# Half of the first matrix product by seven quarter products that share two PSUM banks, and exponentials laid out by key blocks

## The chip, the cores and the metric

The kernel runs on one core of a Trainium2 chip. The metric is the device time of one execution in microseconds (us). Single instructions are given in us or ns. The engines are PE (TensorE; PEld is its weight loads), DVE (VectorE), ACT (ScalarE), POOL (GpSimd) and SP (SyncE, which here only issues DMAs).

## What is computed

All data are float32. `q`, `k`, `v` are 8 batches x 8 heads x 576 rows x 64; the model width is 512, the hidden width 2048.

```python
scores = scale * q @ k.T
thresh = max(scores, -1) - tau
attn = softmax(where(scores >= thresh, scores, -1e9)) @ v
x = attn.transpose(0, 2, 1, 3).reshape(B, S, H * D)     # 8 x 576 x 512
xn = (x - mean(x)) / sqrt(var(x) + 1e-6) * g_ln
out = x + maximum(xn @ w_ch1, 0) @ w_ch2
```

## The kernel before

**Attention** runs in 72 slots (9 to a batch). A slot computes 4 blocks of 128 query rows x 576 keys. PE makes the scores in PSUM (L405). DVE takes the row maxima (L419), ACT makes four exponentials (L432) into a room in SBUF, DVE masks and sums them (L439), and POOL divides (L455). From slot 6 on (`by_blocks`) the weights are turned without PE: two DVE transposes of 32x32 blocks copy the room `e` into a second tile `et` (L529), SP writes `et` to DRAM (L540, four pieces at L536 in the first batch), and reads it back in a new layout as `em` and `er` (L554, L559). The product with the values (L598, L608) is issued in the slot after. From slot 7 on all slots use the same room, `e_room[0]`. A room is free for the next slot's exponentials when it has been copied to `et`.

**The feed-forward part** runs in 16 groups of 288 tokens. The first part (`first_part`) makes 16 feature tiles of 128 x 288: each is 4 products over the model width, one PSUM bank, and one ReLU on ACT (L796) into `hidden`. `product` (L101) issues every product as two of 64 columns; each shows as two PE records, so that a tile has 16 records of 288 columns. Of the rows' scale `rb`, the squares (L802), their sum on POOL (L804) and a `var` product lie among the tiles. In groups 1 to 15 the second part (`second_quarters`) already forms its 2x2 block product by seven quarter products with sums of blocks (the Winograd form of Strassen's method). Each of the seven is a segment of 64 records of 144 columns into one bank, then one ACT copy (L887); sums of blocks are made on DVE and POOL (L872, L912). Group 0's second part is plain. All products of both parts, and `mean` and `var`, take turns in two PSUM banks (tag `ff`).

**The order** is written by hand. A slot is cut in four quarters; `second_part(n, i)` issues as many feed-forward steps as a budget (`ROOM`, `STEPS`) gives to the quarter. PE, ACT, DVE and POOL execute in the order of issue. Quarter 0 follows the scores: maxima, exponentials 0 and 1, the quarter's products, exponentials 2 and 3. The masks and the divisions are issued after quarter 1, the transposes and the DMA after quarter 2, the values' product before quarter 3.

**The start.** The weights arrive as chunks of 512 columns that ACT, DVE and POOL convert (L278 to L313) in the first eleven slots, in spare pieces of SBUF (`Weights`). POOL ends each chunk (L308).

## Time and profile before

| what | value |
|---|---|
| median of 3 runs | 1347.15 us (1347.1 to 1347.81) |
| the profiled execution, first to last instruction | 1345.5 us |
| DVE, ACT, POOL busy, share of the span | 65%, 34%, 46% |
| one maximum, exponential, mask, division | 1351, 754, 810, 792 ns |
| one ReLU of a tile, one copy of a segment | 416, 403 ns |
| one transpose of half a room | 1373 ns |
| DMA of a room to DRAM (L540), issue to landing | 4.8 us (4.1 to 6.5) |

The span is the time from the first to the last instruction of one profiled execution; it lies 1.65 us under the median of the runs. The profile was taken on another execution than the timed ones. Means are over all instructions of a group. PE records overlap, so PE's rate is read from runs of records in the chain of waits and not from the length of one record.

### The profile page before, as it was taken

The numbers are of one execution on the slowest core, as the hardware profiler recorded it, in microseconds if no ns is written. First come the engines' busy times: TensorE is split into PE (matmuls) and PEld (weight loads), VectorE is DVE, ScalarE is ACT, GpSimd is POOL, SyncE is SP. The second block draws the span as 40 slices with busy tenths as digits, with TensorE's granted clock in tenths as the row PEclk, the third lists the DMA queues.
The fourth block names the chain that finished last, engine by engine and source line by source line (L and its number), as shares of the span: only waits on it lengthen the run. The fifth ranks groups of instructions, "written<-read, shape, count | busy, mean of one in ns | idle before, by whom it ended". The sixth has DMA issues, their size and how long they took to land.

```text
span 1345.5 us, 40255 instructions
## 1 busy us (share of the span) xinstructions
PE 1313.5 (98%) x17304; PEld 989.7 (74%) x17304; DVE 870.6 (65%) x1544; ACT 458.7 (34%) x995; POOL 621.9 (46%) x836
## 2 busy tenths in 40 slices
PE   8898899999999999999999999999999999999997
PEld 7665567769686776868778696877869677786957
DVE  7879886667666675666756677656756667666112
ACT  5866333232323233232233324233232323333120
POOL 3475556534444444445535454443444445335312
PEclk9999999999999999999999999999999999999999
DMA  8937874557643775447734576447754476443211
GB/s 173 297 95 176 209 191 151 178 163 190 176 146 132 182 200 158 151 156 200 191 127 150 167 183 191 139 137 196 198 167 152 126 196 179 136 157 124 81 19 20
DMA packets 335298, 213.92 MB, mean 159 GB/s; under 512 B 247376, under 2 KB 292688, under 8 KB 327056
## 3 DMA queue, kind: packets, MB, share of 16 engines
q1 hardware_dynamic: 329008, 210.46, 54.6%
q8 instruction: 136, 2.23, 0.7%
q10 hardware_dynamic: 5952, 0.74, 0.4%
q0 software_dynamic: 160, 0.15, 0.1%
q14 instruction: 42, 0.34, 0.1%
HBM read 124.00 MB, written 87.29 MB: 157 GB/s over the span
## 4 chain that ended last, share of the span: by engine, by line
PE 91%; ACT 3%; DVE 2%; DMA 1%; POOL 1%; issue 1%; SPq 1%; POOLq 0%; ACTq 0%; DVEq 0%
PE p L101 38%; PE seg L101 31%; PE sc L405 10%; PE sc L598 9%; PE sc L608 2%; ACT e L432 1%; PE tp L101 1%; DVE e L439 1%; POOL w L308 1%; PE var L101 1%; PE mean L101 1%; SPq L118 0%; DMA scr<-et 0%; ACT em L489 0%; DMA k_in<-in_k_dram 0%
## 5 line engine op out<-in xcount | busy, mean ns | idle before, releaser
L101 PE MATMUL p<-xc,w 128*64 128x288 f32 x4096 | 517.1, 408 | 6.5 <-ACT part L887 4.6
L101 PEld LDWEIGHTS p<-xc,w 128*64 128x64 f32 x4096 | 287.7, 137 | 213.8 <-issue 13.5
L419 DVE TENSOR_REDUCE neg<-sc 128x2 f32<-128x1152 f32 x144 | 188.7, 1351 | 282.2 <-PE sc L405 281.6
L455 POOL TENSOR_SCALAR e<-e,den 128x576 f32<-128x576 f32 x264 | 205.9, 792 | 131.3 <-DVE den L444 131.3
L101 PE MATMUL seg<-hidden,w 128*64 128x144 f32 x3840 | 247.9, 287 | 0.0
L101 PEld LDWEIGHTS seg<-hidden,w 128*64 128x64 f32 x3840 | 234.9, 137 | 11.5 <-issue 8.5
L439 DVE SCALAR_TENSOR_TENSOR e<-sc,thr,e 128x576 f32<-128x576 f32 x288 | 222.4, 810 | 19.3 <-POOL thr L423 11.6
L423 POOL TENSOR_SCALAR thr<-neg,low_sb 128x2 f32<-128x2 f32 x144 | 39.4, 274 | 384.1 <-DVE neg L419 382.4
L796 ACT ACTIVATE hidden<-p 128x288 f32<-128x288 f32 x256 | 106.5, 416 | 305.3 <-PE p L101 303.7
L432 ACT ACTIVATE e<-sc,neg 128x576 f32<-128x576 f32 x288 | 197.6, 754 | 2.4 <-DVE neg L419 2.4
L529 DVE STREAM_TRANSPOSE et<-e 128x1152 f32<-128x1152 f32 x118 | 161.1, 1373 | 14.2 <-POOL e L455 13.7
L405 PE MATMUL sc<-kT,qT 64*64 64x384 f32 (+3 forms) x2048 | 140.3, 403 | 3.1 <-DVE e L439 3.1
L598 PE MATMUL sc<-em,v_in 128*64 128x128 f32 (+1 forms) x2368 | 130.9, 264 | 2.4 <-DVE w L293 2.4
L598 PEld LDWEIGHTS sc<-em,v_in 128*64 128x64 f32 x2368 | 124.0, 138 | 10.9 <-DVE w L293 2.6
L101 PE MATMUL seg<-hidden,stage 128*64 128x144 f32 x1920 | 123.3, 286 | 0.0
L101 PEld LDWEIGHTS seg<-hidden,stage 128*64 128x64 f32 x1920 | 117.6, 137 | 2.9 <-issue 2.9
L621 ACT COPY x<-sc 128x128 f32<-128x128 f32 x120 | 31.6, 265 | 245.2 <-PE sc L405 176.3
L405 PEld LDWEIGHTS sc<-kT,qT 64*64 64x64 f32 x2048 | 76.3, 133 | 44.6 <-issue 21.3
L872 POOL TENSOR_TENSOR hidden<-hidden 128x576 f32<-128x576 f32 x60 | 84.8, 1427 | 52.0 <-ACT hidden L796 42.4
L887 ACT COPY part<-seg 128x288 f32<-128x288 f32 x74 | 29.8, 403 | 190.6 <-PE seg L101 190.1
L872 DVE TENSOR_TENSOR hidden<-hidden 128x576 f32<-128x576 f32 x60 | 51.2, 887 | 51.5 <-PE seg L101 48.5
L101 PE MATMUL seg<-hidden,e 128*64 128x144 f32 x896 | 61.2, 286 | 0.0
(130 smaller groups left out, 1041.2 us busy)
## 6 DMA issues: line engine op xcount, KB each, us to landing
scr<-et SPq DMA_DIRECT2D x63, 1152.0 KB, 4.8
em<-scr SPq DMA_DIRECT2D x63, 1024.0 KB, 5.7
out_dram<-ot SPq DMA_DIRECT2D x248, 36.0 KB, 3.8
q_in<-in_q_dram SPq DMA_DIRECT2D x120, 72.0 KB, 2.7
er<-scr SPq DMA_DIRECT2D x132, 64.0 KB, 5.2
k_in<-in_k_dram SPq DMA_DIRECT2D x116, 72.0 KB, 3.0
v_in<-in_v_dram SPq DMA_DIRECT2D x28, 256.0 KB, 5.4
w<-in_moe_w_ch_dram SPq DMA_DIRECT2D x10, 512.0 KB, 7.0
```

The costliest lines, as they stand in the source:

```text
L101: nc.tensor.matmul(out[r], lhsT=lhsT[:, r], rhs=rhs, **flags)
L405: nc.tensor.matmul(sc[h][64 * i : 64 * i + 64, at : at + n], lhsT=ql[r] if s == HP else qT[r, half, j * 128 + 64 * i : j * 128 + 64 * i + 64],
L419: nc.vector.tensor_reduce(out=neg[:, i], in_=pairs[h], axis=AXL.X, op=ALU.max, negate=True,)
L423: nc.gpsimd.tensor_scalar(out=thr[:, i], in0=neg[:, i], scalar1=-1.0, scalar2=low_sb, op0=ALU.mult, op1=ALU.add,)
L432: nc.scalar.activation(es[:, i], blocks[i], func=AF.Exp, bias=neg[:, i : i + 1])
L439: nc.vector.scalar_tensor_tensor(out=es[:, i], in0=blocks[i], scalar=thr[:, i : i + 1], in1=es[:, i], op0=ALU.is_ge, op1=ALU.mult, accum_o ...
L455: nc.gpsimd.tensor_scalar(out=es[:, i], in0=es[:, i], scalar1=den[:, i : i + 1], scalar2=1.0, op0=ALU.mult, op1=ALU.mult,)
L529: nc.vector.transpose(et[:, :, 64 * h : 64 * h + 64].rearrange("p n (j c) -> p j n c", j=2), es[:, 2 * h : 2 * h + 2].rearrange("p j (n c) ...
L598: nc.tensor.matmul(dst[64 * h : 64 * h + 64], lhsT=vt[:, h, c, :], rhs=pick(em[:, 2 * j : 2 * j + 2, c], h), start=c == 0 and first, stop= ...
L621: nc.scalar.copy(x_of(2 * b + (s > HP))[:, s % (HP + 1), 128 * j : 128 * j + 128], pv[j])
L796: nc.scalar.activation(hidden[:, d], p1, func=AF.Relu)
L872: eng.tensor_tensor(out=out[at], in0=in0[at], in1=in1[at], op=op)
```

## The change

**Products.** In groups 2 to 15, feature tiles 4 to 7 and 12 to 15 are no longer made one by one. `chain` runs after the other eight tiles and makes them in two passes of four tiles. A pass is seven segments of 16 records of 144 columns (two tiles, half the model width, half the tokens). Two segments use a bank of their own afresh; the others add onto what stands in one of the pass's two banks, so that most of the sums of the method are made by PE's accumulation. After each segment ACT copies the bank out, and the segment after the next, in the same bank, needs that copy done. Three of a pass's four output blocks need one more term; POOL adds it and applies the ReLU (`rectify`). Four sums of input blocks per group (`turns`, two on DVE, two on POOL) are issued two tiles before the chain. Sums of the weights' blocks (`chain_sums`) are made once, during group 1's second part.

**Attention.** The room is laid out by blocks of 32 keys: an exponential writes runs of 32 elements, 128 apart. The two transposes write where they read, `et` is gone, and SP writes the room itself to DRAM. While a chain runs, the exponentials are issued one behind each segment's copy (`held`), and the copy of one bank of values is issued after quarter 0.

**Room.** `chain_sb` takes the place of `et` as a place for weight chunks (three pieces, for all chunks; `et` gave two, for the first 13). `e_room[1]` is handed to the weights one slot later. `qT` is two tiles with 2 and 4 buffers. The budget counts the shorter groups.

```diff
...
@@ -88,7 +88,18 @@
     er_sb = consts.tile([128, 2, 128], F32, name="er")
     v_rest = [consts.tile([128, 2, 2, D], F32, name=f"v_rest{i}") for i in range(HP)]
     hidden = consts.tile([128, ND, TOK], F32, name="hidden")
-    e_room = [consts.tile([128, 4, S], F32, name=f"e{i}") for i in range(2)]
+    e_room = [consts.tile([128, 4 * S], F32, name=f"e{i}") for i in range(2)]
+    CHAIN = list(range(4, 8))
+    CW = 128 * len(CHAIN)
+    chain_sb = consts.tile([128, 3, 2, CW], F32, name="chain_sb")
+    def by_rows(e):
+        return e.rearrange("p (i s) -> p i s", i=4)
+    def by_columns(e):
+        return e.rearrange("p (n i c) -> p i n c", i=4, c=32)
     units = [(b, hp) for b in range(B) for hp in range(HP)]
     loaded, values_in, turned = {}, {}, {}
...
@@ -224,7 +234,7 @@
                 (hidden, 4, lambda p: 10),
                 (x_room, 1, lambda p: 2 * n1),
                 (y_room, 1, lambda p: 2 * n1),
-                (et_room, 2, lambda p: n1 - 3),
+                (chain_sb.rearrange("p a k c -> p (a k) c"), 3, lambda p: 2 * n1),
                 (stage, 4, lambda p: 2 * n1),
             ):
                 for p in range(n):
...
@@ -424,12 +438,13 @@
                 out=thr[:, i], in0=neg[:, i], scalar1=-1.0, scalar2=low_sb,
                 op0=ALU.mult, op1=ALU.add,
             )
-            if h == 0:
+            if h == 0 and not chained[0]:
                 run(n, "copy")
         for i in range(4):
-            if i == 2:
-                yield es, thr
-            nc.scalar.activation(es[:, i], blocks[i], func=AF.Exp, bias=neg[:, i : i + 1])
+            yield room, es, thr
+            nc.scalar.activation(
+                es[:, i], as_in(es, blocks[i]), func=AF.Exp, bias=neg[:, i : i + 1]
+            )
     def weights(es, thr, divide):
...
@@ -515,21 +530,13 @@
             )
         yield em, er
-    def turn_blocks(b, s, es):
-        et = att.tile([128, NB, 128], F32, tag="et", bufs=1, name="et")
-        if s == HP:
-            nc.vector.transpose(
-                et.rearrange("p n (u c) -> p u n c", u=HP),
-                es.rearrange("p u (n c) -> p u n c", c=32),
-            )
-        else:
-            for h in range(2):
-                nc.vector.transpose(
-                    et[:, :, 64 * h : 64 * h + 64].rearrange("p n (j c) -> p j n c", j=2),
-                    es[:, 2 * h : 2 * h + 2].rearrange("p j (n c) -> p j n c", c=32),
-                )
+    def turn_blocks(b, s, room):
+        et = room.rearrange("p (n x) -> p n x", x=128)
+        for h in range(2):
+            two = et[:, :, 64 * h : 64 * h + 64]
+            nc.vector.transpose(two, two)
         scr = dram.tile([4, S, 128], F32, tag="scr", name="scr")
         if b == 0:
             for a in range(4):
...
@@ -773,18 +780,132 @@
                     eng.tensor_tensor(out=out[at], in0=a[at], in1=b[at], op=op)
                     yield
+    def chain_sums():
+        cols = slice(128 * CHAIN[0], 128 * CHAIN[0] + CW)
+        low = slice(DF // 2 + cols.start, DF // 2 + cols.stop)
+        s2, s3, s4 = (chain_sb[:, i] for i in range(3))
+        for k in range(2):
+            a11, a12 = w1_sb[k][:, cols], w1_sb[k + 2][:, cols]
+            s1, a22 = w1_sb[k][:, low], w1_sb[k + 2][:, low]
+            for eng, out, a, b, op in (
+                (nc.gpsimd, s3[:, k], a11, s1, ALU.subtract),
+                (nc.vector, s1, s1, a22, ALU.add),
+                (nc.vector, s2[:, k], s1, a11, ALU.subtract),
+                (nc.gpsimd, s4[:, k], a12, s2[:, k], ALU.subtract),
+            ):
+                eng.tensor_tensor(out=out, in0=a, in1=b, op=op)
+                yield
+    chained = [False]
+    def chain(g, xc):
+        drip(everything=True)
+        turns = ffn.tile([128, NK, TOK], F32, tag="sq", bufs=1, name="turns")
+        t1, t2, t3, t4 = (
+            turns[:, 2 * i : 2 * i + 2, cols] for i in range(2) for cols in (early, late)
+        )
+        b11, b12, b21, b22 = (
+            xc[:, 2 * i : 2 * i + 2, cols] for i in range(2) for cols in (early, late)
+        )
+        for eng, out, a, b, op in (
+            (nc.vector, t3, b22, b12, ALU.subtract),
+            (nc.vector, t2, t3, b11, ALU.add),
+            (nc.gpsimd, t1, b12, b11, ALU.subtract),
+            (nc.gpsimd, t4, b21, t2, ALU.subtract),
+        ):
+            eng.tensor_tensor(out=out, in0=a, in1=b, op=op)
+        yield
+        low = DF // 2
+        w1 = lambda k, at: lambda c, d: w1_sb[k + c][:, at + d * 128 : at + d * 128 + 128]
+        sums = lambda i: lambda c, d: chain_sb[:, i, c, (d - CHAIN[0]) * 128 : (d - CHAIN[0] + 1) * 128]
+        a11, a12, s1, a22 = w1(0, 0), w1(2, 0), w1(0, low), w1(2, low)
+        s2, s3, s4 = (sums(i) for i in range(3))
+        def segment(bank, weights, rhs, ds, first):
+            for i, d in enumerate(ds):
+                for c in range(2):
+                    at, end = (i, c), (len(ds) - 1, 1)
+                    product(
+                        bank[:, i], lhsT=weights(c, d), rhs=rhs[:, c],
+                        start=first and at == (0, 0), stop=at == end,
+                        skip_group_check=not first,
+                    )
+                    if at != end:
+                        yield 1, 0.5
+        def rectify(eng, t, other):
+            eng.tensor_tensor(out=t, in0=t, in1=other, op=ALU.add)
+            eng.tensor_scalar(
+                out=t, in0=t, scalar1=0.0, scalar2=1.0, op0=ALU.max, op1=ALU.mult
+            )
+        for n, at in enumerate(range(0, len(CHAIN), 2)):
+            ds = CHAIN[at : at + 2]
+            banks = [ps_ff.tile([128, 2, HT], F32, tag="ff", name="ch") for _ in range(2)]
+            one, two = banks if n % 2 == 0 else banks[::-1]
+            up, down = (hidden[:, ds[0] + o : ds[0] + o + 2] for o in (0, ND // 2))
+            m1, u2, m7 = (None,) * 3
+            part_tile = lambda name: ffn.tile([128, HM, HT], F32, tag="part", bufs=4, name=name)
+            chained[0] = True
+            yield from segment(one, a11, b11, ds, True)
+            m1 = part_tile("m1")
+            nc.scalar.copy(m1, one)
+            yield 2, 0.5
+            yield from segment(two, a12, b21, ds, True)
+            nc.scalar.copy(up[:, :, early], two)
+            rectify(nc.gpsimd, up[:, :, early], m1)
+            yield 2, 0.5
+            yield from segment(one, s2, t2, ds, False)
+            u2 = part_tile("u2")
+            nc.scalar.copy(u2, one)
+            yield 2, 0.5
+            yield from segment(two, s3, t3, ds, True)
+            m7 = part_tile("m7")
+            nc.scalar.copy(m7, two)
+            yield 2, 0.5
+            yield from segment(one, s1, t1, ds, False)
+            if n == 1:
+                while len(rooted) <= g:
+                    run_all(aside)
+            nc.scalar.copy(down[:, :, late], one)
+            rectify(nc.gpsimd, down[:, :, late], m7)
+            yield 2, 0.5
+            yield from segment(two, a22, t4, ds, False)
+            nc.scalar.copy(down[:, :, early], two)
+            rectify(nc.gpsimd, down[:, :, early], u2)
+            yield 2, 0.5
+            yield from segment(one, s4, b22, ds, False)
+            nc.scalar.activation(up[:, :, late], one, func=AF.Relu)
+            if at + 2 >= len(CHAIN):
+                chained[0] = False
+            yield 2, 0.5
     def first_part(g):
         xc = centred.pop(g)
         rb = sq = None
         plain = g == 0
+        in_chain = CHAIN if g > 1 else []
+        tiles = [d for d in range(ND) if d % (ND // 2) not in in_chain]
+        last = len(tiles) - 1
         sums_of = differences() if g == 1 else iter(())
-        for d in range(ND):
+        if g == 2:
+            for _ in later_sums:
+                pass
+        chains = chain(g, xc) if in_chain else None
+        for t, d in enumerate(tiles):
             while conversion.carried < 4 * (d // 4 + 1):
                 yield 0, 0
             while d == ND - 2 and len(rooted) <= g and not plain:
                 run_all(aside)
+            if chains and t == last - 1:
+                next(chains)
             p1 = ps_ff.tile([128, TOK], F32, tag="ff", name="p1")
             for c in range(NK):
                 product(
@@ -796,15 +917,15 @@
             nc.scalar.activation(hidden[:, d], p1, func=AF.Relu)
             next(sums_of, None)
             yield 2, 1
-            if sq is None and d and (part > 1 or d == ND // 2 - 1):
-                squared = d
+            if sq is None and t and (part > 1 or t == (4 if chains else ND // 2 - 1)):
+                squared = t
                 sq = hidden[:, ND - NK :]
                 nc.scalar.activation(sq, xc, func=AF.Square)
                 for c in range(1, NK):
                     nc.gpsimd.tensor_tensor(out=sq[:, 0], in0=sq[:, 0], in1=sq[:, c], op=ALU.add)
             elif sq is not None and rb is None and (
-                d >= squared + (7 if plain else 3) and part > (0 if plain else 1)
-                or d == ND - NK - 1
+                t >= squared + (7 if plain else 3) and part > (0 if plain else 1)
+                or t == (last if chains else ND - NK - 1)
             ):
                 var = ps_ff.tile([128, TOK], F32, tag="ff", name="var")
                 product(var, lhsT=avg_sb, rhs=sq[:, 0], start=True, stop=True)
@@ -820,7 +941,11 @@
                 yield 1, 1
         for _ in sums_of:
             pass
+        if chains:
+            yield from chains
         return rb
+    later_sums = chain_sums()
     def second_plain(g, rb):
         for m in range(NK):
...
@@ -982,11 +1109,12 @@
     ROOM = (0.6, 1.0, 1.25, 0.35)
-    STEPS = [1 + NK * ND * 2] + [1 + NK * ND * 2 - NK * ND // 8] * (NG - 1)
+    STEPS = [1 + NK * ND * 2 - (NK * ND // 8 if g else 0) - (len(CHAIN) if g > 1 else 0) for g in range(NG)]
     ends = [sum(STEPS[: i + 1]) for i in range(NG)]
     queue = []
     issued = part = now = 0
     owed = 0.0
+    held = iter(())
     later_calls = {}
     def at_quarter(n, i, fn, *args):
@@ -1029,6 +1157,8 @@
                 issued += cost
                 owed -= cost
                 steps += 1
+                if chained[0] and got == 2:
+                    next(held, None)
                 if steps == 4 and among:
                     mean_of(among[0])
                     centre(among.pop())
@@ -1098,20 +1228,26 @@
         if n + 1 < HP:
             scale_q(n + 1, loaded[n + 1][0])
         rest = exponentials(n)
-        es, thr = next(rest)
+        room, es, thr = next(rest)
+        for _ in range(0 if chained[0] else 2):
+            next(rest)
         conversion.carry_all()
         run(n, 0)
         if n == HP + 2:
+            next(rest)
             next(rest, None)
         if n >= HP:
             conversion.fetch(1 if n == FIRST + 2 else 3, -1 if n > FIRST else 1)
         run_first(stores)
         if early_at(n):
             convert(masks_at)
+        held = rest
         second_part(n, 0)
+        run(n, "copy")
         while drops and drops[0][0] is nc.gpsimd:
             drops.pop(0)[-1]()
-        next(rest, None)
+        while not chained[0] and next(held, None):
+            pass
         u = (n + 1) // SLOTS * HP + (n + 1) % SLOTS
         if (n + 1) % SLOTS < HP and u < len(units):
@@ -1130,6 +1266,8 @@
             conversion.prepare_to(behind_at, False)
         run(n, 1)
         second_part(n, 1)
+        while next(held, None):
+            pass
         if n > FIRST:
             conversion.prepare_to(behind_at, False)
         blocks_go = by_blocks(n)
@@ -1147,11 +1285,9 @@
         if blocks_go:
             conversion.fetch(0 if n == FIRST + 2 else 3, wait=0)
             conversion.prepare_to(end_at, False)
-            scr = turn_blocks(b, s, es)
+            scr = turn_blocks(b, s, room)
             if n == FIRST:
-                conversion.take(e_room[1])
-            if n == FIRST:
-                conversion.fetch(3)
+                at_quarter(n + 1, 0, conversion.take, e_room[1])
             conversion.carry_all()
             at_quarter(n + 1, 0, lambda b=b, s=s, scr=scr, box=box: box.append(fetch(b, s, scr)))
         else:
```

More of the change, by code (lines that the diff above doesn't have):

```diff
@@ L213, in __init__ @@
             y_room = ffn.tile([128, NK, TOK], F32, tag="sq", bufs=1, name="y_room")
-            et_room = att.tile([128, NB, 128], F32, tag="et", bufs=1, name="et_room")
             stage = self.stage = consts.tile([128, 8, WC], F32, name="stage")
@@ L236, in take @@
         def take(self, t):
-            t = t.rearrange("p a b -> p (a b)")
             for p in range(2):
@@ L352, in turn @@
             scale_q(u, q_in)
-        qT = att.tile([128, 2, QH], F32, tag="qT", bufs=4, name="qT")
+        qT = [att.tile([128, QH], F32, tag=f"qT{s}", bufs=2 + 2 * s, name=f"qT{s}") for s in range(2)]
         kT = att.tile([128, S], F32, tag="kT", bufs=4, name="kT")
@@ L360, in turn @@
                 nc.vector.transpose(
-                    qT[:, s].rearrange("p (j a c) -> p a j c", j=2, a=4),
+                    qT[s].rearrange("p (j a c) -> p a j c", j=2, a=4),
                     part.rearrange("p (a j) c -> p a j c", j=2),
@@ L364, in turn @@
             else:
-                nc.vector.transpose(qT[:, s], part.rearrange("p n c -> p (n c)"))
+                nc.vector.transpose(qT[s], part.rearrange("p n c -> p (n c)"))
         nc.vector.transpose(
@@ L406, in scores, with as_in @@
                     sc[h][64 * i : 64 * i + 64, at : at + n],
-                    lhsT=ql[r] if s == HP else qT[r, half, j * 128 + 64 * i : j * 128 + 64 * i + 64],
+                    lhsT=ql[r] if s == HP else qT[half][r, j * 128 + 64 * i : j * 128 + 64 * i + 64],
                     rhs=kT[r, o : o + n], start=True, stop=True,
                 )
+    def as_in(es, block):
+        return block if len(es.shape) == 3 else block.rearrange("p (n c) -> p n c", c=32)
     def exponentials(n):
@@ L415, in exponentials @@
         thr = small.tile([128, 4], F32, tag="thr", name="thr")
-        es = e_room[(n + 1) % 2 if n <= FIRST else 0]
+        room = e_room[(n + 1) % 2 if n <= FIRST else 0]
+        es = by_columns(room) if by_blocks(n) else by_rows(room)
         for h in range(2):
@@ L439, in weights @@
             nc.vector.scalar_tensor_tensor(
-                out=es[:, i], in0=blocks[i], scalar=thr[:, i : i + 1], in1=es[:, i],
+                out=es[:, i], in0=as_in(es, blocks[i]), scalar=thr[:, i : i + 1], in1=es[:, i],
                 op0=ALU.is_ge, op1=ALU.mult, accum_out=den[:, i : i + 1],
@@ L541, in turn_blocks @@
             out=scr.rearrange("a (r n) x -> (a r) (n x)", r=32),
-            in_=et.rearrange("p n x -> p (n x)"),
+            in_=room,
         )
@@ L757, in differences @@
         flat = conversion.stage.rearrange("p a b -> p (a b)")
-        flat4 = e_room[1].rearrange("p a b -> p (a b)")
+        flat4 = e_room[1]
         size = HM * HD * 128
@@ L887, in segment @@
             nc.scalar.copy(out, bank)
+            if g == 1:
+                next(later_sums, None)
             return out
```

## The prediction

> **What bounds the kernel now.** I read the busy shares first, then busy time by stretch, then the chain of waits, then the timeline around two places.
>
> ```profile
> PE 1313.5 (98%) x17304; PEld 989.7 (74%) x17304; DVE 870.6 (65%) x1544; ACT 458.7 (34%) x995; POOL 621.9 (46%) x836
> ```
>
> PE is nearly always busy. By stretch (start and end, length, then busy time of PE, PEld, DVE, ACT, POOL, the granted clock, the DMA share and GB/s):
>
> ```profile
> 0.00:80.00 80.00, 70.13 (x1070) 55.67 (x1071) 64.58 (x131) 56.58 (x118) 35.93 (x61) 1.00 0.86 226
> 80.00:175.00 95.00, 85.05 (x824) 51.56 (x826) 80.99 (x142) 46.42 (x90) 58.28 (x62) 0.98 0.66 161
> 175.00:250.00 75.00, 74.97 (x1038) 56.93 (x1035) 54.28 (x89) 23.78 (x54) 44.18 (x53) 1.00 0.57 171
> 250.00:1243.00 993.00, 988.65 (x13122) 746.61 (x13120) 650.50 (x1143) 316.03 (x696) 454.79 (x633) 1.00 0.56 165
> 1243.00:1345.50 102.50, 94.71 (x1264) 78.94 (x1260) 20.25 (x43) 15.87 (x39) 28.70 (x29) 0.99 0.18 41
> ```
>
> From 250 to 1243 us PE idles 4.35 of 993 us: what PE no longer issues there comes off the end, as long as no new wait fills the place. From 80 to 175 us PE idles 10 of 95 us and DVE is at 81 of 95: there the conversion of the weights is in the way.
>
> PE's rate stands in the chain of waits (start, length, what):
>
> ```profile
> 253.29 1.00 PE seg L101 x16
> 254.29 0.02 issue
> 254.31 0.04 ACTq L887
> 254.35 0.04 issue
> 254.39 0.41 ACT part L887
> 254.80 0.04 issue
> 254.84 5.56 PE p L101 x44
> ...
> 279.21 1.94 PE p L101 x16
> ...
> 297.01 0.98 PE seg L101 x16
> ```
>
> Sixteen records of 288 columns, one old tile, take 1.94 us; sixteen of 144 columns, one new segment, 0.98 us. The first lines show the hand-over that the change will need all the time: sixteen records, a copy, and the next product in that bank starts 254.84 - 253.29 = 1.55 us after the first record's place in the chain. In the timeline of the same hand-over in a later group the first of the sixteen starts at 728.39, the copy at 729.67 and the waiting product at 730.12: 1.73 us in all, of which the copy starts after 1.28. I use the longer. The sixteenth record starts 0.87 us after the first, so that 0.86 us is the way from a bank's last record to its next user.
>
> **The products.** A group from 2 on loses 8 tiles x 1.94 = 15.52 us of PE and gains 14 segments x 0.98 = 13.72 us: 1.80 us less. Fourteen groups: **-25.2 us**. All of it is PE's own time, which sets the end in this stretch and in the last 102 us. PEld is no new bound at 144 columns: its groups show 61 ns a load against 64.5 ns a record in the second part's segments, which have this form already.
>
> **The hand-over.** Two segments lie between a bank's use and its reuse: 2 x 0.98 = 1.96 us, against the 1.73 needed. The slack is 0.23 us, if ACT is free on time. What may stand before a copy is an exponential. The timeline of ACT shows how closely they follow:
>
> ```profile
> 706.05 1.38 ACT L432 ACTIVATE e<-sc,neg 128x576 f32<-128x576 f32 x2
> ...
> 707.31 0.41 ACT L887 COPY part<-seg 128x288 f32<-128x288 f32 x1
> 707.59 1.41 ACT L432 ACTIVATE e<-sc,neg 128x576 f32<-128x576 f32 x2
> ```
>
> Two exponentials take 1.38 us, 0.69 each, and one starts 0.28 us after a copy has started. Copy and exponential thus fill 0.97 us of a segment's 0.98: no delay builds up. The first exponential waits for its maximum, 1.65 us after PE left the scores (its next product is at 704.40, the exponential at 706.05). Counted from 704.40 the first segment's copy is due at 1.28 and the second's at 2.26 us; the exponential between them is through at 1.65 + 0.69 = 2.34. By these rows the chain costs nothing. Above nothing it can cost 0.69 us for each of 4 exponentials in one slot per group, if every copy meets the whole of one: 14 x 4 x 0.69 = 38.6 us. I take 0.2 us a group, **+3 us**, for the ends of quarters and the `var` product, because the sum of the rows lies at nothing. Six more copies a group (14 for 8 ReLUs; 2.4 us) lie on ACT, 34% busy.
>
> **POOL and DVE.** A `rectify` is a sum of 288 elements (0.80 us by the rows of L912) and a scale of 288 (about 0.50, between 474 ns for 256 and 532 for 320 on L338). Six, and two sums of 0.80: 9.4 us a group. In the two stretches where the chains will lie POOL is busy 5.1 of 20.6 us (672.4 to 693.0) and 7.9 of 21.8 (750.2 to 772.0), so they fit. The second part needs the last rectified block one 3.9 us segment later and its first POOL sum (2 x 1.42) two segments later. If this cover goes, each us of POOL's lag past it is a us of PE. Thresholds and divisions queue behind the rectifications on POOL, the masks of DVE behind the thresholds; `neg` and `thr` are issued ahead of the chain, and the scores that wait for the masks come some 9 us after them (710.8 to 720.2). DVE's two sums (0.46 each) come two tiles, 3.9 us, and two segments before their use. The eight weight sums (four of 1.28 us on POOL, four of 0.68 on DVE) lie beside group 1's second part. I take nothing for all of this.
>
> The Trainium skill speaks against this part in "SBUF — State Buffer", section "Who interferes with whom": a DVE operation with two SBUF inputs and a GpSimd operation that reads SBUF lock each other out for a whole instruction. The trace agrees that they disturb each other: L872 on DVE has a median of 752 ns and a maximum of 1957. By the rule some DVE sums would be a whole POOL instruction later; the sum stays, since DVE is not what PE waits for.
>
> **Layout and transposes.** The strided forms are not in the trace for all engines. The nearest rows: the strided copy of 512 elements (L489) takes 593 ns, a plain exponential of 576 takes 754, and the turned copy already goes in runs of 32. So nothing per exponential, mask and division; one gives or takes 0.1 us at most, off PE's path. The seven slots with one transpose of 2.58 us get two of 1.37.
>
> **The new wait** is that of the next exponentials for the DMA of the room, which `et` used to carry. Issue of the DMA to the next first exponential is 6.3 us or more from 242 us on (699.74 to 706.05 is the tightest kind); the DMA lands after 4.8, at most 6.5. So nothing there. In the first slots it is otherwise:
>
> ```profile
> 118.10 3.82 SPq L536 DMA_DIRECT2D scr<-et  x4
> ...
> 119.51 1.38 ACT L432 ACTIVATE e<-sc,neg 128x576 f32<-128x576 f32 x2
> ...
> 120.76 0.42 ACT L796 ACTIVATE hidden<-p 128x288 f32<-128x288 f32 x1
> ```
>
> The four pieces are issued until 121.9 and land 4.6 us later (median of L536), the last at 126.3 in the trace: the exponential of 119.51 comes 6.8 us late. Behind it on ACT stand the ReLUs of the last two tiles, for which PE's next product waits, and the low words of three chunks (L283), for which POOL waits. The same reckoning gives lateness of 3.3 us at 142.0, 1.2 at 164.7, 2.5 at 184.8, 0.9 at 201.7, none at 217.3 and 1.5 at 233.0: 16.2 us in all. PE doesn't lose all of it: it loses 6.3 at 121.7, but two later idle times (2.35 us at 130.5 until DVE's masks, 4.07 at 150.1 until POOL) have their cause on DVE and swallow about 3; at 142.0 ACT's next copy for PE has a slack of some 8 us, and I let about 1.5 reach PE through POOL; 0.6 at 164.7; at 184.8 the tile's slack of 1.94 - 0.86 = 1.1 us leaves 1.4; the rest is inside that slack. Sum 6.8, **+7 us**. Bounds: 16.2 above; below, the 10 us that PE idles from 80 to 175 us could go, since `chain_sb` gives more places for chunks than `et` and the fetches move.
>
> The Trainium skill adds a price here, in "TensorE: Matmul & The Clock Gate", Part 1: after about 3.4 us of idleness TensorE runs the next 3.4 us at half clock. The rows show 0.98 granted in the stretch with the 4.07 us wait. One such cooling would add about 1.7 us, an estimate from that page.
>
> **Sum.** 1345.5 - 25.2 + 3 + 7 = 1330.3 us for the span; the median of the runs stood 1.65 above: **1332 us**, 1.1% less.
>
> **The rivals.**
> 1. The start costs nothing and the chains run without a stall: 1347.15 - 25.2 = 1322, down to 1316 if part of the start's idle time goes too. For it: the rows of the hand-over sum to no stall. Against: the DMA lands late in seven slots.
> 2. The gain is eaten up. The start at its upper bound (16) and 0.5 us of stall a group (7): 1347.15 - 25.2 + 23 = 1345, no change. For it: lateness adds up from slot to slot, since a later exponential makes a later DMA.
> 3. Slower: the hand-over in the chains falls out of step with ACT. Each copy of a slot's four exponentials waits a whole exponential: 38.6 us, with the start's 7 that is 1347.15 - 25.2 + 45.6 = 1368. It decides from (25.2 - 7) / 56 = 0.33 us per exponential, or 0.09 us per segment over the slack of 0.23 us (196 segments). For it: the slack is thin, and POOL's backlog could hold back the four `part` buffers that the copies write. Against: copy and exponential fit a segment by the rows above.
> 4. The change doesn't do what it says: the segments are held by loads at 1.11 us for 0.98 (1.80 / 14 = 0.13 more each), and nothing is saved. Time 1347 or more. Against: 6720 records of that form run at that rate.
>
> **Chances.** Forecast (1324 to 1340) 0.52; rival 1 (under 1324) 0.16; rival 2 (1340 to 1352) 0.14; rival 3 (over 1352) 0.15; rival 4 0.03. A difference of 0.2% is 2.7 us, about what a measurement of this kernel can tell from none. Faster: the first two and about a third of rival 2, 0.73; within 0.2%: 0.09; slower: 0.18. The range takes in rivals 1 and 2 and leaves rival 3 out: 1316 to 1352.
>
> **What would show it.** 14 x 224 = 3136 records of 144 columns more, and 14 x 128 = 1792 of 288 columns fewer. In the chain of waits segments `ch` of sixteen at 0.98 us with no ACT piece between them; an ACT copy or POOL piece there speaks for rival 3. In the stretch from 250 us on PE's idle time stays near 4 us. At the start PE waits for ACT near 121 us for about 6 us and the exponentials of slot 8 for the room's DMA. I'm wrong if idle time from 250 us on grows by over 10 us, or if the 80 to 175 us stretch gets shorter.

## The result, and the profile after

The changed kernel takes 1366.99 us (median of 4 runs, 1365.66 to 1369.73) against 1347.15: the ratio is 1.0151, with a 95% interval of 1.0137 to 1.0166. It is 1.5% slower; the forecast was 1.1% faster, with a range that ended at 1352. The profiled execution took 1367.19 us, of which the span is 1365.1.

PE does less work and the end comes later. The busy line of the page after:

```profile
PE 1300.3 (95%) x18648; PEld 1055.0 (77%) x18648; DVE 908.4 (67%) x1583; ACT 489.7 (36%) x1079; POOL 816.0 (60%) x1036
```

PE has 18648 records, 1344 more than before: 14 x 224 = 3136 new ones less 14 x 128 = 1792 old ones, as predicted. So the products were exchanged. POOL has 194 us more. The stretches (PE, PEld, DVE, ACT, POOL busy; granted clock, DMA share, GB/s):

```profile
80.00:175.00 95.00, 83.27 (x790) 50.07 (x792) 78.54 (x130) 45.89 (x89) 56.55 (x60) 0.95 0.60 149
175.00:250.00 75.00, 71.63 (x894) 52.15 (x892) 53.26 (x99) 22.85 (x50) 44.24 (x51) 1.00 0.54 158
250.00:1243.00 993.00, 961.41 (x14230) 795.79 (x14228) 669.39 (x1148) 334.74 (x753) 612.71 (x797) 1.00 0.55 164
```

From 250 to 1243 us PE idles 31.6 us, where it was 4.35. To hold runs against each other, I add up for each stretch what the distance between the starts of neighbouring PE records has over the usual one (the median) for their form. This is PE's lost time, in us, worked out from each trace:

| stretch | before | after | e1 | e15 | e6 | e9 |
|---|---|---|---|---|---|---|
| 80 to 175 | 13.5 | 17.4 | 17.8 | 12.8 | 16.7 | 14.8 |
| 175 to 250 | 1.0 | 5.0 | 3.0 | 1.0 | 4.7 | 2.6 |
| 250 to 1243 | 17.4 | 52.8 | 17.6 | 17.5 | 42.3 | 30.2 |
| whole span | 48.2 | 92.6 | 53.8 | 46.9 | 79.6 | 62.8 |

After less before is 44.4 in all; less the 25.2 us that the products save this is 19.2, and the span grew by 19.6. So the saving is there, the start (80 to 250 us) costs 7.9 us, and the groups in the steady part (250 to 1243 us) lose 35.4 us. The waits of PE name where (total, times, longest):

```profile
PE ch L112 <- ACT hidden L917: 11.2, 6, 2.0
PE p L112 <- ACT hidden L917: 6.5, 2, 5.9
PE sc L605 <- DVE e L454: 5.6, 6, 1.1
...
PE ch L112 <- ACT hidden L875: 4.0, 7, 1.0
```

The second line is the start, where the next product waits 5.9 us for a ReLU. The others recur in the groups; I call them A (first line), C (third) and B (fourth). Wait A in the timeline of an odd group:

```profile
681.92 0.84 DVE L723 STREAM_TRANSPOSE ot<-y 128x288 f32<-128x288 f32 x2 [3.54 <-POOL y L1039]
...
683.55 0.84 DVE L723 STREAM_TRANSPOSE ot<-y 128x288 f32<-128x288 f32 x2 [0.80 <-POOL y L1039]
684.43 0.46 DVE L821 TENSOR_TENSOR turns<-xc 128x288 f32<-128x288 f32 x1
...
684.92 0.95 DVE L821 TENSOR_TENSOR turns<-turns,xc 128x288 f32<-128x288 f32 x1
685.79 2.61 DVE L433 TENSOR_REDUCE neg<-sc 128x2 f32<-128x1152 f32 x2
...
687.33 1.38 ACT L445 ACTIVATE e<-sc,neg 128x576 f32<-128x576 f32 x2
...
688.59 0.42 ACT L917 ACTIVATE hidden<-p 128x288 f32<-128x288 f32 x1
...
689.06 1.20 PE L112 MATMUL ch<-xc,w 128*64 128x144 f32 x16 [1.83 <-ACT hidden L917]
```

`chain` starts with `drip(everything=True)`, which issues all waiting output transposes at once, and with the turn sums. On DVE these stand ahead of the maxima, the transposes themselves waiting for POOL. PE's next product after the scores starts at 684.59 and the maxima at 685.79; the exponentials behind them on ACT come late, behind those stands the ReLU of the last ordinary tile, and the first segment needs the bank that it empties. From the start of the `var` product (686.58) to that of the segment 2.48 us pass.

Waits B and C are in the even groups. For B the same transposes and sums stand between the maxima and the masks, so the room goes to DRAM late, and the next slot's exponential waits for it:

```profile
757.30 2.62 DVE L433 TENSOR_REDUCE neg<-sc 128x2 f32<-128x1152 f32 x2 [6.78 <-PE sc L414]
...
764.20 0.81 DVE L454 SCALAR_TENSOR_TENSOR e<-sc,thr,e 128x576 f32<-128x576 f32 x1
...
770.62 0.34 SPq L547 DMA_DIRECT2D scr<-e  x1
...
775.70 0.74 ACT L445 ACTIVATE e<-sc,neg 128x576 f32<-128x576 f32 x1 [1.12 <-DVE neg L433]
776.34 0.39 ACT L875 COPY hidden<-ch 128x288 f32<-128x288 f32 x1
```

The exponential starts 2.66 us after its maximum, where 1.55 is usual, and the copy for the seventh segment is behind it. The trace names the maximum as releaser, but that began at 773.04 and takes 1.35 us; what ended last is the room's DMA, issued at 770.62, with a median of 5.0 us to landing. For C, the q scale stands on POOL behind rectifications that wait for ACT's copies, and DVE, which waits for it, reaches the masks late:

```profile
781.61 0.75 POOL L347 TENSOR_SCALAR q_in<-q_in,scl_sb 128x576 f32<-128x576 f32 x1
782.39 0.77 DVE L369 STREAM_TRANSPOSE qT<-q_in 128x256 f32<-128x256 f32 x2 [6.04 <-POOL q_in L347]
...
783.21 0.78 DVE L454 SCALAR_TENSOR_TENSOR e<-sc,thr,e 128x576 f32<-128x576 f32 x1
...
786.45 1.75 PE L605 MATMUL sc<-em,v_in 128*64 128x128 f32 x28 [0.81 <-DVE e L454]
```

In the chain's own course there is no such wait: in that group segments start at 777.82, 779.86, 781.82 and 783.78, two in 1.96 us or a little more, which is 0.98 each.

A wait can cost more than its length. Behind wait A of the group at 849 us the granted clock of TensorE is 0.50 from 850.5 to 853.9 us, where pairs of records come every 0.24 us and not 0.123; 1.5 us are lost there (worked out like the lost time). In the steady part of the change this is the only such stretch; some of the runs below have more of them.

**The theory** (queue order): the change puts work ahead of other work on in-order queues, and PE meets the delay at A, B, C and at the start. **The rival** (hand-over): a segment of 0.98 us leaves ACT too little time beside exponentials, which is the prediction's third rival and gave 1368.

### The profile page after: what moved, and what is told of

The parts are those of the page before. It is cut to its first block, busy times and chain, and to the rows that moved or that the text cites. A ratio compares the mean times of both kernels' runs of the same rounds, so it can differ in the third digit from the quotient of the medians.

```text
span 1365.1 us, 43424 instructions
## 1 busy us (share of the span) xinstructions
PE 1300.3 (95%) x18648; PEld 1055.0 (77%) x18648; DVE 908.4 (67%) x1583; ACT 489.7 (36%) x1079; POOL 816.0 (60%) x1036
## 5 line engine op out<-in xcount | busy, mean ns | idle before, releaser
L112 PE MATMUL p<-xc,w 128*64 128x288 f32 x2304 | 292.5, 408 | 8.2 <-ACT part L1012 4.0
L470 POOL TENSOR_SCALAR e<-e,den 128x576 f32<-128x576 f32 x264 | 200.0, 770 | 104.3 <-DVE den L459 104.3
L112 PEld LDWEIGHTS p<-xc,w 128*64 128x64 f32 x2304 | 162.1, 137 | 126.2 <-issue 11.1
L445 ACT ACTIVATE e<-sc,neg 128x576 f32<-128x576 f32 x288 | 201.8, 754 | 38.8 <-DMA scr<-e 34.2
L539 DVE STREAM_TRANSPOSE e<-e 128x1152 f32<-128x1152 f32 x132 | 180.4, 1374 | 41.8 <-POOL e L470 40.8
L917 ACT ACTIVATE hidden<-p 128x288 f32<-128x288 f32 x144 | 59.7, 415 | 157.1 <-PE p L112 155.5
L843 POOL TENSOR_SCALAR hidden<-hidden 128x288 f32<-128x288 f32 x84 | 99.6, 1185 | 7.7
L997 DVE TENSOR_TENSOR hidden<-hidden 128x576 f32<-128x576 f32 x60 | 57.8, 999 | 38.6 <-POOL hidden L997 20.9
```

The costliest lines, as they stand in the source:

```text
L112: nc.tensor.matmul(out[r], lhsT=lhsT[:, r], rhs=rhs, **flags)
L445: nc.scalar.activation(es[:, i], as_in(es, blocks[i]), func=AF.Exp, bias=neg[:, i : i + 1])
L470: nc.gpsimd.tensor_scalar(out=es[:, i], in0=es[:, i], scalar1=den[:, i : i + 1], scalar2=1.0, op0=ALU.mult, op1=ALU.mult,)
L539: nc.vector.transpose(two, two)
L843: eng.tensor_scalar(out=t, in0=t, scalar1=0.0, scalar2=1.0, op0=ALU.max, op1=ALU.mult)
L917: nc.scalar.activation(hidden[:, d], p1, func=AF.Relu)
```

## The experiments

Times are medians; the kernel before, run on the same chip, took 1346.4 to 1346.9 us. In the expectations theory A is the queue order, theory B the hand-over, and theory C, where it is spelled out, the room in place; these letters are not those of the waits.

### The start

**e1**, no quarter products and no weight sums, only the layout:

```diff
...
-        in_chain = CHAIN if g > 1 else []
+        in_chain = []
...
```

> The new layout with transposes in place stays; the chains are off (all sixteen tiles by single products, as before; the weight sums are not made). Theory A (the loss has two parts: about 8 us at the start from the room's DMA, and about 2.5 us per group of waits that arise only where chain, POOL, DVE and ACT queues meet): about 1355 us, with PE's idle time from 250 us on near the 4 us of before. Theory B (rival 3 as it stood in the prediction: the hand-over from PE to ACT in the chains is too slow for the segments): the same 1355 or less. Theory C (the room in place delays the exponentials in every slot, chains or not): 1380 to 1392, the full loss of 20 us and the 25 us that the chains should have saved.

Measured 1352.53 us, ratio 1.0041 (1.0026 to 1.0056). The steady part loses what it lost before (17.6 against 17.4), so nothing of A, B and C comes from the layout by itself.

**e2**, the change with the second room kept for exponentials (one block of weights then stands in for a weight sum that had its place there):

```diff
...
-        room = e_room[(n + 1) % 2 if n <= FIRST else 0]
+        room = e_room[(n + 1) % 2]
...
```

> The changed kernel with the two rooms in turn for all slots, so that no exponential waits for the DMA of the slot before. For that the second room is taken from the weights' chunks and from one of the second part's weight sums, whose products read another block of weights instead: that part of the computation is not the reference's. Theory A: the start's 8 us and the waits of about 0.9 us in every other group (6 us) go, the waits at the chain's head stay: about 1353 us. Theory B: only the start goes, about 1359 us. Theory C: 1330 us or less.

Measured 1358.67 us, 1.0079 (1.0062 to 1.0096). The start's wait and B are gone, A stays (11.0 us in six waits) and C too (6.6). That the median is theory B's 1359 and not theory A's 1353 doesn't speak against the queue order: in the profile four stretches of the steady part at a granted clock of 0.50 lose 6.4 us, against 1.5 in the change.

**e15**, e1 and e2 together:

> The layout alone (1352.5), but the exponentials of all slots alternate between two rooms, so that none waits for the DMA of the slot before. For it the second room isn't given to weights: a block of the second part's weights stands where one of their sums should. Wait theory (the layout costs only by exponentials waiting for the room's DMA in the first slots): 1347 (1345.5 to 1348.5). Form theory (strided exponentials, masks and in-place transposes are slower themselves): 1350 to 1353, no change.

Measured 1346.51 us, 1.0000 (0.9990 to 1.0009). The layout costs nothing but the wait for the room's DMA; the strided forms are free, as predicted.

**e10**, e1 with slot 8's exponentials behind the first quarter's products:

```diff
...
-        for _ in range(0 if chained[0] else 2):
+        for _ in range(0 if chained[0] or n == FIRST + 2 else 2):
```

> No quarter products and no weight sums, only the exponentials by key blocks in one room, with the four exponentials of slot 8 issued behind the first quarter's products instead of ahead of them. Queue theory: of the 5.7 us that the layout alone cost, the 6 us wait of a tile for its ReLU at the start is most, because the ReLU stands behind an exponential that waits for the room's DMA; it goes, and 1348 is left (1346 to 1350). Rival (the exponentials being late at all is what costs, through masks and transposes that come later): the time stays at 1351 to 1353.

Measured 1350.30 us, 1.0026 (1.0016 to 1.0035): 2.2 of the 5.7 us go, less than the 4.5 expected. The wait of 5.9 us is gone from the list; a wait of 4.1 us for POOL's last conversion, which before had and e1 had not, is back. So late exponentials also cost by what comes after them, and the rival named there has a part.

### The groups

**e5**, the next slot's q scale ahead of the quarter's rectifications:

```diff
-        if not 0 < u < HP:
+        if u == 0:
             scale_q(u, q_in)
...
         conversion.carry_all()
+        u = (n + 1) // SLOTS * HP + (n + 1) % SLOTS
+        if (n + 1) % SLOTS < HP and HP <= u < len(units):
+            scale_q(u, loaded[u][0])
         run(n, 0)
```

> The changed kernel, with the scaling of the next slot's q issued on POOL ahead of quarter 0's products and not behind that quarter's rectifications. Theory A says that in every other group the values' product waits about 1 us for the masks because DVE stood at the transposes of q, which stood behind rectifications on POOL. That wait goes: 7 x 1 us, about 1360 us. If POOL's backlog does not reach PE this way, 1367 us.

Measured 1362.62 us, 1.0118 (1.0102 to 1.0135). C leaves the list of waits; the gain is 4.4 us, not the 7 expected. Behind five of its six waits A the granted clock is 0.50, and 7.9 us are lost there, against 1.5 in the change; the mean clock is 0.989 to 0.990 in all four runs, and was 0.992 to 0.994.

**e6**, the forced output transposes and turn sums one tile later, in even groups behind the block transposes:

```diff
...
-            if chains and t == last - 1:
-                next(chains)
+            if chains and t == last:
+                if part == 2:
+                    pending.append(lambda: chain_inputs(xc, cell))
+                else:
+                    chain_inputs(xc, cell)
...
             scr = turn_blocks(b, s, room)
+            while pending:
+                pending.pop()()
```

> The changed kernel, with the sums of the chain's inputs (and the finishing of the group before, which they force out first) issued at the last tile, and behind the room's transposes where that tile lies in quarter 2. Theory A: in even groups the room's transposes and its DMA come some 4 us earlier, the next exponentials no longer wait for that DMA, and the wait of about 0.9 us at the chain's seventh segment goes (6 us); in odd groups the maxima start 1.2 us earlier and the wait at the chain's head falls from 2.8 to about 1.7 us (8 us): about 1353 us. Theory B (hand-over): no change, 1367 us.

Measured 1354.53 us, 1.0058 (1.0041 to 1.0075): 12.5 us from this order alone. In the group that answers to the one shown for B, maxima, masks and DMA are at 750.66, 753.68 and 760.13: 9.5 us from the maxima to the DMA, not 13.3. A falls to 0.7 us at most (4.5 in six waits).

**e13**, on the change, exponentials of a slot that begins in the last ordinary tile behind that tile's ReLU:

```diff
             nc.scalar.activation(hidden[:, d], p1, func=AF.Relu)
+            if chains and t == last - 1:
+                chained[0] = True
```

> The change with one edit: the exponentials of a slot that begins in the last ordinary tile are issued one at each hand-over from then on, so they stand behind that tile's ReLU on ACT and not ahead of it. Queue theory: the first segment's wait of 2.0 us goes in the six or seven odd groups that have it, 10 to 14 us less: 1355 (1352 to 1358). Rival (the exponentials cost the same wherever they stand, as the move of the variance product showed for its wait): the wait comes back at a later segment and the time stays at 1364 to 1368.

Measured 1358.35 us, 1.0089 (1.0072 to 1.0105). Wait A's 11.2 us leave the list; 8.6 us are gained, just short of the 10 expected; B grows from 4.0 to 5.3 us.

**e4**, e5, e10's move, a `var` product one tile earlier, turn sums one tile later and the rectification's steps swapped, all in one:

> The changed kernel with five moves and no other computation: the exponentials of slot 8 after that quarter's products; the swapped rectification; the var product one tile earlier; the sums of the chain's inputs one tile later; the scaling of the next q ahead of quarter 0's products. Theory A: most of the 2.5 us per group and 6 us of the start go: 1367 - 28 to 1367 - 38, that is 1330 to 1339 us. Theory B: the segments are still too fast for ACT: about 1358 us. Theory C: 1360 us.

Measured 1364.19 us, 1.0126 (1.0111 to 1.0142), a miss: C went and the start shrank, but in even groups the sums, now behind the masks, still stood ahead of the room's transposes (in the group that answers to B's 14.6 us pass from the maxima to the DMA, 752.30 to 766.93), and B grew to 2.2 us a group. Four stretches at a clock of 0.50 behind it lose 6.2 us more.

**e7**, `var` two tiles before the end:

```diff
-                t >= squared + (7 if plain else 3) and part > (0 if plain else 1)
-                or t == (last if chains else ND - NK - 1)
+                t >= squared + (7 if plain else 2 if chains else 3) and part > (0 if plain else 1)
+                or t == (last - 2 if chains else ND - NK - 1)
```

> The changed kernel, with the var product two tiles earlier, so that the chain's first two banks are not those of the last tile's ReLU and of var's copy, which stand behind exponentials on ACT. Theory A: in odd groups the wait at the chain's head falls from 2.8 us to about 1.3 us, 10 us in all: about 1357 us. Theory B: 1367 us.

Measured 1388.90 us, 1.0308 (1.0292 to 1.0323): much worse. The first segment waits no longer, but the second waits up to 2.7 us for the same ReLU in odd groups, and the seventh up to 2.5 us for its copy in even ones. An even group and an odd one:

```profile
612.89 0.44 DVE L744 SCALAR_TENSOR_TENSOR hidden<-rb 128x288 f32<-128x288 f32 x1
...
615.09 2.62 DVE L539 STREAM_TRANSPOSE e<-e 128x1152 f32<-128x1152 f32 x2
...
622.86 0.74 ACT L445 ACTIVATE e<-sc,neg 128x576 f32<-128x576 f32 x1 [2.67 <-DMA scr<-e]
623.49 0.39 ACT L875 COPY hidden<-ch 128x288 f32<-128x288 f32 x1
...
693.64 0.45 DVE L744 SCALAR_TENSOR_TENSOR hidden<-rb 128x288 f32<-128x288 f32 x1
...
695.46 2.61 DVE L433 TENSOR_REDUCE neg<-sc 128x2 f32<-128x1152 f32 x2
```

With `var` the three DVE operations that finish the rows' scale (L744 to L748) come earlier too. In odd groups they stand ahead of the maxima, which start 2.3 us after PE's next product (693.14) and not 1.2; in even groups ahead of the room's transposes, so the DMA is issued at 617.74, the next exponential waits for it, and the copy for the seventh segment stands behind that. The wait has moved, as the hand-over theory has it, but the rows show once more work put ahead on a queue. Besides, seven stretches at a clock of 0.50 behind these waits lose 11.5 us.

**e8**, e5, e6, e7 and e10's move:

> The three moves of this call together, and the exponentials of slot 8 behind that quarter's products. Theory A: 1367 less 7, 14 and some 5 of what the moves share in odd groups, and 4 at the start: about 1340 us, a little faster than the kernel before. Theory B: 1360 us.

Measured 1355.24 us, 1.0058 (1.0039 to 1.0077), a miss by 15 us. C is gone from the list and A small, and a new wait heads it:

```profile
PE ch L112 <- DVE turns L822: 11.1, 7, 1.6
```

The third segment waits in even groups. In the one whose chain starts at 601.84, PE could begin it when the second is through, some 0.9 us after 604.81; but the turn sums, behind the room's transposes and the output transposes, only start at 605.73, and the segment at 607.30. Here it does matter when the sums come.

**e9**, e5, e6, e10's move and e13's, `var` left in its place:

> Three edits that each put work later or earlier on an in-order queue, and leave all arithmetic as the change has it: the turn sums behind the block transposes (as in the run that had them alone, 1354.5), the q scale of the next slot ahead of the quarter's rectifications, the four exponentials of slot 8 behind the quarter's products; and in addition the exponentials of a slot that begins in the last ordinary tile go behind the ReLU of that tile. Queue theory (PE waits for work that stands behind other work on ACT, DVE and POOL): the values' wait of about 1 us in even groups goes (-4.4 to -6), the start loses 4 us, and the 2 us wait of the first segment in odd groups goes (seven of them, -10): 1336, between 1332 and 1342, faster than before. Hand-over theory (a segment of 0.98 us leaves ACT too little time, wherever the exponentials stand): the waits move to other segments and the time stays at 1350 to 1356.

Measured 1340.19 us (1338.12 to 1341.8), ratio 0.9946 (0.9933 to 0.9958): faster than both kernels, with the change's arithmetic untouched. The place of A in its timeline:

```profile
670.09 2.62 DVE L433 TENSOR_REDUCE neg<-sc 128x2 f32<-128x1152 f32 x2 [0.29 <-PE sc L414]
...
672.20 0.41 ACT L932 ACTIVATE hidden<-p 128x288 f32<-128x288 f32 x1 [1.78 <-PE p L112]
672.50 0.73 ACT L445 ACTIVATE e<-sc,neg 128x576 f32<-128x576 f32 x1
672.63 0.45 DVE L822 TENSOR_TENSOR turns<-xc 128x288 f32<-128x288 f32 x1
672.66 2.39 PE L112 MATMUL ch<-xc,w 128*64 128x144 f32 x32
```

Maxima directly behind the scores, the ReLU ahead of the exponentials, the sums behind the maxima: the segment starts 0.68 us after `var` (671.98), not 2.48.

**e14**, e9 without e13's edit:

> The faster kernel (1340.2) without that one edit, so turn sums behind the transposes, q scale ahead of the rectifications, slot 8's exponentials behind the quarter's products. Queue theory: the first segment's wait of about 0.9 us that the run with the sums alone still had in odd groups comes back, and with it the variance product's Identity ahead of the copy: 1340.2 + 6 = 1346 (1344 to 1349). Rival: no more than 1342, the other three edits did it.

Measured 1344.97 us, 0.9985 (0.9975 to 0.9996). That edit is worth 4.8 us beside the others, the other three 22.

### The hand-over and POOL

**e11**, the change with all four exponentials of a slot at its start also while a chain runs:

```diff
-        for _ in range(0 if chained[0] else 2):
-            next(rest)
+        for _ in range(4 if chained[0] else 2):
+            next(rest, None)
```

> The change, with all four exponentials of a slot issued at its start also while the chains run, instead of one at each hand-over. Queue theory: copies for two segments then stand behind up to 2.8 us of exponentials, so the two segments after them wait about 1.5 to 2 us in each of 14 groups: 1367 + 21 to 28 = 1388 to 1395. Hand-over theory in the form the prediction's third rival gave it (each copy meets one exponential and pays for it): in a row they meet only two copies, not four, so the time falls by up to 10 us: 1357 to 1367.

Measured 1411.47 us, 1.0479 (1.0465 to 1.0494), more than either theory said. Its waits:

```profile
PE ch L112 <- ACT m L869: 40.1, 13, 4.8
PE ch L112 <- ACT hidden L917: 11.2, 6, 2.0
```

The second line is A, unchanged. The first is new: 3.1 us a group for a copy behind four exponentials. Ten stretches of the steady part at a clock of 0.50 lose another 16.0 us. One exponential between two copies costs the chain next to nothing, a row of them costs more than the products save.

**e3**, the two operations of the rectification in the other order (times one, then maximum with zero):

> The changed kernel with the two operations of the rectification's second POOL instruction swapped (times 1, then the maximum with 0). If the 1185 ns of it come from the maximum being the first operation, it falls to about 500 ns, POOL is 57 us less busy, and by theory A the values' product no longer waits for the masks behind POOL (about 1 us in every other group): about 1360 us. If it stays at 1185 ns, 1367 us. Theory B: 1367 us either way.

Measured 1367.55 us, 1.0150 (1.0134 to 1.0165), no change. The operation takes what it took:

```profile
L843 POOL TENSOR_SCALAR hidden<-hidden 128x288 f32<-128x288 f32 x84 | 99.5, 1185 | 7.7
```

**e12**, e9 without that operation:

> As the run with the order on the queues changed, but the second step of each rectification (the maximum with zero on POOL, 1.19 us for 288 elements, 84 of them) is left out, so six of eight tiles' quarter sums are not rectified. It takes 99.6 us from POOL. If POOL's length of work still reaches PE: 4 to 10 us less than that run. If only the order on the queues mattered: within 2 us of it.

Measured 1342.30 us, 0.9958 (0.9943 to 0.9973), not to be told from e9. POOL's busy time falls from 820.7 to 721.4 us and PE gains nothing.

## Why the prediction was wrong

**The products, -25.2: right.** The rate of 0.98 a segment held, and spans and lost time close on it: for e6, 79.6 - 48.2 - 25.2 = 6.2, and its span of 1351.8 is 6.3 above before's; for the change 19.2 against 19.6; for e9 -10.6 against -9.2.

**The start, +7: right in size,** at 7.9 in the trace and 5.7 us by e1. The stall at slot 8 was predicted at 6.3 and is 5.9. One part was too small, PE's clock. The rows of the stall (stretch, length, PE busy and records, granted clock, DMA share, GB/s):

```profile
121.90:127.70 5.80, 0.00 (x0) 0.93 0.78 197
127.70:131.00 3.30, 3.25 (x14) 0.50 1.09 302
131.00:134.20 3.20, 3.20 (x18) 0.58 1.07 229
```

Pairs of records come every 0.48 us until 133.87, and then every 0.243: 13 pairs, so 3.1 us more. The Trainium skill ("TensorE: Matmul & The Clock Gate", Part 1) puts the slow time at one busy window of about 3.4 us or more. The trace has both: 0.50 from 126.9 to 133.7, twice 3.4, behind this wait, and 3.4 us at 850.5. The 1.7 us that I had estimated from that page fits the second, where 1.5 were lost, and is too small for the first.

**Layout and transposes, nothing: right** (e15).

**The steady part is where it failed: 35.4 us against 3.** The step is the sentence "I take nothing for all of this" in POOL and DVE, with its reason that DVE's two turn sums come "two tiles, 3.9 us, and two segments before their use". That is true of the change, and answers only half of the question: the cost came from what stands behind the sums. I had reckoned neither the output transposes that `drip(everything=True)` issues with them, nor that they wait for POOL, nor that maxima, masks and the room's DMA are next on DVE. I also reckoned that thresholds and divisions queue behind rectifications, and forgot the q scale, which does so too. Edits of order alone, e9, take back 26.8 us of the median; in PE's lost time that is 22.6 us of the steady part's 35.4 and 5.0 at the start. I also put a clock that falls behind waits in the groups at nothing; it is 1.5 us in the profiled run of the change.

**The new wait, "nothing there": wrong** in the groups. I took the tightest distance from issue to next exponential, 6.3 us, from the trace of before, but the masks and transposes that lead to the issue are themselves moved by the change. In the trace after the distance is 775.70 - 770.62 = 5.1.

**The hand-over, +3: the size was off.** In e9, with A, B and C gone or small, the steady part still loses 30.2 - 17.4 = 12.8 us, 0.9 a group against 0.2. The largest pieces are 0.58 at the fifth segment in each of six groups, whose copy stands behind two exponentials, and 0.28 on average at the third in 13; for seven of these the list names the turn sums on DVE and not a copy. So the hand-over has at most what is left, and how much of it was not tried apart. That 1368 was hit by rival 3 is a coincidence: it asked for 56 exponentials each paid in full, and in the change's chains segments run at 0.98 us beside them. Its core, that a copy behind exponentials stalls PE, is true where several come in a row (e11) or where one comes late itself (B, e7).

**POOL, 9.4 us a group: the size was off.** The rectification's second step takes 1185 ns and not "about 0.50", so six rectifications and two sums take about 6 x 2.0 + 1.8 = 13.8 us. By e12 that step's 99 us do not reach PE once the order is mended; the one way on which the rows show the rectifications reaching PE is C. The mutual hindrance of DVE and POOL that I dismissed because "DVE is not what PE waits for" lies on the way to A: the second turn sum takes 0.95 us beside POOL's sum, the first, which starts before POOL's, 0.46. The Trainium skill's lock ("SBUF — State Buffer", section "Who interferes with whom") would have it so; no run here separates that half microsecond from the rest of A.

**Open:** e7 is read from its rows alone; no run moves `var` without the operations behind it. When a wait brings the clock down was not tried either: in e7 it does in seven of 13 groups. That e9 is still 8 us above the 1332 forecast adds up: 9.8 more in the steady part than the 3 allowed, 4.1 less at the start than the 7, and 2.2 because the profiled execution (1338.12, span 1336.3) was the fastest of the five, so that the median stands 3.9 above that span and not 1.65.

## What to carry to other kernels

Of work that is issued earlier, ask what stands behind it on its engine and what it waits for itself, and then whether it comes in time (when moved later, too: e8); follow that from queue to queue until PE or a DMA. Where an engine executes in order and feeds another through two buffers, a saving in the product is worth only what the order of the small operations lets through: here the same arithmetic gave +20 or -6.5 us. A wait that is taken away alone often shows up one place on (e4, e7, e8), so move the cause, which stands further up the chain of queues.

## What the runs showed of the hardware

- On POOL a `tensor_scalar` of maximum and multiplication took 1185 ns for 288 elements in either order; the multiplication alone had taken 532 ns for 320. Which of the two operations, or the layout of the tile, makes the difference was not tried.
- After 5.9 us without products TensorE's granted clock was 0.50 for 6.8 us (126.9 to 133.7), beyond the wait itself 3.1 us lost.
- Behind single waits of 2.0 to 2.7 us (e4, e7) it was 0.50 for 3.4 us in some groups, 1.4 to 1.7 us lost each time, and 1.00 in others with as long a wait.
- Exponentials that write runs of 32 elements, and transposes in place, take what the plain forms take (754 and 1374 ns after, 754 and 1373 before).
